# Output projection of an attention and S4D stack: float16 pairs with scales in place of split float32 pairs, and the normalised stream from ScalarE

## Chip, cores and metric

The kernel runs on one core of one Trainium2 chip. The metric is the device time of one execution in microseconds (us), the median over the runs shown. The profiler took one execution apart; times inside it count from the start of its span. Engines: PE is TensorE, PEld its weight loads, DVE is VectorE, ACT is ScalarE, POOL is GpSimd, SP is SyncE; SPq and POOLq are the queues from which SP and POOL issue transfers.

## What is computed

A stream x of 2048 rows by 640 columns goes through four layers, two of them attention (A) and two a state-space convolution (B), with the same weights each time:

```python
x = x + _A_ref(_layernorm(x), A_wqkv, A_wo)
x = x + _B_ref(_layernorm(x), B_log_A_real, B_A_imag, B_C_real, B_C_imag, B_log_dt, B_D_skip)
x = x + _A_ref(_layernorm(x), A_wqkv, A_wo)
x = x + _B_ref(_layernorm(x), ...)
```

A is attention with 32 heads of 20 columns: softmax of the scaled scores, times the values, and the result o, 2048 by 640, times the matrix wo, 640 by 640. That last product is the output projection, and it is what the change edits. B builds one filter of length 2048 for each of the 640 channels, convolves each channel with it by way of Fourier transforms, and adds the skip term.

## The kernel before

Rows of x are spread so that partition p holds rows 16p to 16p+15; a "row" s, 0 to 15, is one slice of 128 rows by 640 columns. A layer pair is attention (with the projection at its end), then the convolution, ssm; this happens twice, and the text calls them layer 1 and layer 2.

**Attention** runs blocks of four heads and 512 queries, 32 blocks a layer. Each block is 32 score tiles S of 128 by 1024 (scores, L769), one exp on ScalarE each into pt (L772), and the products of pt with the values into pa (values, L786), a pair of PSUM banks that exists once. At the end of a block VectorE copies pa to oc and adds the second bank (oc). The row sums then go through memory to be inverted and spread: POOL issues dn (four small stores from oc), dr (a load), VectorE inverts dr, POOL issues dn (a store) and db (four loads that spread it), VectorE multiplies oc by db, and POOL issues ot (four stores). Each of these steps has a due time in a planner's clock (the list later), and the wrapper Ordered (L74, the line that most VectorE, POOL and SP instructions carry) ties VectorE's instructions, and the transfers of POOL and SP, in the order in which they are recorded. POOL's arithmetic isn't tied: there a scheduler chooses the place.

**end_jobs** is called once a layer, when the side jobs of the attention are done. In layer 2 it checks the range of the weights wqkv by a maximum over all partitions (partition_all_reduce on POOL) and then calls **prefetch**, which loads wo into five tiles wot of 128 by 640 and splits each on POOL into two float32r halves: woh by a cast (L925), wol by a subtraction (L926). In layer 1 it loads x as well, in four transfers. POOL can hold the code of its arithmetic or that of the all-reduce; where it changes, the order of the instructions shows a row ISA with no operands.

**out_split** prepares one row of the attention's result: a load otl, a cast oh on ScalarE (L943), a subtraction ol on VectorE. **out_proj** takes the 16 rows in turn: for each half of 320 columns 15 matmuls into po (ol by woh, L1035; oh by woh and by wol, L1041), and VectorE adds po to x. Every two rows, and singly for the last two, ln_u makes the layer norm's output for the convolution: statistics on VectorE, u = (x - mean) * rs on VectorE, uh (float16) on ScalarE (L956), ul = u - uh on POOL (L957), for the last row on VectorE. The convolution's first matmuls (psx, L1100) read uh and ul. In layer 1 the transform of the filters, ktransform, is woven between the rows from row 2 on: it loads kl for 128 channels at a time, transposes and transforms (pkt, pkx, pkf), with copies out of PSUM on ScalarE and VectorE.

Line numbers are those of the profile.

## Time and profile before

| | before |
|---|---|
| median of 3 runs | 2904.78 us (2903.93 to 2905.59) |
| the profiled execution | 2906.51 us |
| its span | 2904.60 us |
| PE busy | 2581.2 us, 89% |
| ACT busy | 2360.6 us, 81% |
| DVE busy | 1497.7 us, 52% |
| POOL busy | 795.5 us, 27% |
| mean granted clock of TensorE | 0.98 |

The span is the time between the first and the last instruction on the core; 1.91 us of the execution lie outside it. A busy share is an average over the whole program, which has stages with different limits: in the attention loops ScalarE works without a pause, in the projections and the convolutions TensorE does. What a stage is worth is read from the stretch itself.

### The profile page before, as it was taken

The numbers are of one execution on the slowest core, as the hardware profiler recorded it, in microseconds if no ns is written. First come the engines' busy times: TensorE is split into PE (matmuls) and PEld (weight loads), VectorE is DVE, ScalarE is ACT, GpSimd is POOL, SyncE is SP. The second block draws the span as 40 slices with busy tenths as digits, with TensorE's granted clock in tenths as the row PEclk, the third lists the DMA queues.
The fourth block names the chain that finished last, engine by engine and source line by source line (L and its number), as shares of the span: only waits on it lengthen the run. The fifth ranks groups of instructions, "written<-read, shape, count | busy, mean of one in ns | idle before, by whom it ended". The sixth has DMA issues, their size and how long they took to land.

```text
span 2904.6 us, 127995 instructions
## 1 busy us (share of the span) xinstructions
PE 2581.2 (89%) x57088; PEld 1537.6 (53%) x57088; DVE 1497.7 (52%) x3333; ACT 2360.6 (81%) x2862; POOL 795.5 (27%) x1229
## 2 busy tenths in 40 slices
PE   7679898998999788789999898999999978878999
PEld 3235555554555444367788554544444433334988
DVE  8555667777775687146777633332222200001865
ACT  5878888998899788855565488999999989998364
POOL 1002223222222222330067012222222332222376
PEclk9889999999999999999999999999999999999999
DMA  5212222222111111335454212121211211112265
GB/s 165 105 55 58 62 59 60 62 53 68 52 55 42 51 41 50 131 119 185 190 188 140 67 35 64 55 65 40 61 46 44 66 28 39 31 43 61 86 204 162
DMA packets 174754, 231.45 MB, mean 80 GB/s; under 512 B 35952, under 2 KB 124336, under 8 KB 172400
## 3 DMA queue, kind: packets, MB, share of 16 engines
q1 hardware_dynamic: 139856, 180.84, 19.2%
q0 software_dynamic: 34336, 42.32, 5.8%
q8 instruction: 450, 7.37, 1.1%
q14 instruction: 112, 0.92, 0.1%
HBM read 150.94 MB, written 72.10 MB: 77 GB/s over the span
## 4 chain that ended last, share of the span: by engine, by line
ACT 26%; PE 18%; issue 6%; DMA 3%; DVE 2%; POOL 1%; SPq 0%; ACTq 0%; POOLq 0%; DVEq 0%
ACT pt L772 25%; PE psv L1135 2%; PE psy L1145 2%; PE po L1041 2%; PE psx L1123 2%; PE psx L1100 2%; PE pst L1110 1%; PE pkf L1015 1%; PE pkx L998 1%; PE pv L524 1%; PE po L1035 1%; PE pa L786 1%; PE pq L682 1%; DMA kl<-kd 1%; PE pkt L1007 1%
## 5 line engine op out<-in xcount | busy, mean ns | idle before, releaser
L772 ACT ACTIVATE pt<-S 128x1024 f32<-128x1024 f32 x2048 | 1932.4, 1040 | 168.2 <-PE S L769 155.1
L786 PE MATMUL pa<-pt,V 64*32 64x512 f32 x16384 | 1144.3, 597 | 17.3 <-DVE oc L74 9.3
L769 PE MATMUL S<-qop,kop 61*32 61x512 f16 x16384 | 921.8, 383 | 184.6 <-ACT pt L772 149.1
L769 PEld LDWEIGHTS <-kop 61*32 61x32 f16 x16384 | 393.8, 90 | 836.9 <-issue 742.5
L786 PEld LDWEIGHTS pa<-pt,V 64*32 64x32 f32 x16384 | 330.1, 107 | 93.7 <-issue 32.0
L74 POOL DMA_DIRECT2D dn<-oc x256 | 126.2, 499 | 446.2 <-DVE oc L74 352.4
L74 POOL DMA_DIRECT2D ot<-oc x256 | 129.2, 512 | 392.5 <-DVE oc L74 313.3
L74 DVE TENSOR_SCALAR qc<-m 128x512 f32<-128x512 f32 x64 | 44.2, 690 | 298.9 <-PE m L560 298.8
L322 PE MATMUL m<-kb,ka 64*32 64x64 f32 x10240 | 158.4, 222 | 44.6 <-issue 42.4
L322 PEld LDWEIGHTS m<-kb,ka 64*32 64x32 f32 x10240 | 150.8, 105 | 82.4 <-issue 65.3
L74 DVE COPY oc<-pa 128x512 f32<-128x512 f32 x64 | 44.2, 691 | 275.0 <-PE pa L786 275.0
L74 POOL DMA_DIRECT2D db<-dn x256 | 128.5, 508 | 133.7 <-DMA dn<-dr 126.0
L74 DVE TENSOR_TENSOR kb<-ktab 128x512 f32<-128x512 f32 x240 | 155.9, 684 | 16.4 <-PE m L322 16.4
L560 PE MATMUL m<-xh,wh 64*32 64x512 f16 x2560 | 148.8, 382 | 12.5 <-DVE qc L74 12.5
L560 PE MATMUL m<-xl,wh 64*32 64x512 f16 x2560 | 148.0, 381 | 0.0
L560 PE MATMUL m<-xh,wl 64*32 64x512 f16 x2560 | 147.0, 380 | 0.2 <-issue 0.2
L560 PEld LDWEIGHTS <-wh 64*32 64x32 f16 x5120 | 97.1, 94 | 79.0 <-issue 42.2
L1128 POOL TENSOR_TENSOR t<-t,kb 128x512 f32<-128x512 f32 x80 | 101.9, 1274 | 71.2 <-DVE t L74 70.3
L1112 ACT COPY xt<-pst 128x1024 f16<-128x1024 f16 x80 | 81.6, 1023 | 46.7 <-PE pst L1110 46.5
L74 DVE TENSOR_SCALAR dr<-dr 128x16 f32<-128x16 f32 x64 | 14.7, 229 | 188.5 <-DMA dr<-dn 188.4
L74 DVE TENSOR_TENSOR oc<-oc,db 128x512 f32<-128x512 f32 x64 | 44.1, 690 | 125.7 <-DMA db<-dn 124.2
L74 POOL DMA_DIRECT2D dn<-dr x64 | 35.6, 556 | 263.8 <-DVE dr L74 256.7
(222 smaller groups left out, 3877.3 us busy)
## 6 DMA issues: line engine op xcount, KB each, us to landing
ka<-kha SPq DMA_DIRECT2D x80, 256.0 KB
kb<-khb SPq DMA_DIRECT2D x80, 256.0 KB
db<-dn POOLq DMA_DIRECT2D x256, 64.0 KB, 2.6
qop<-qs SPq DMA_DIRECT2D x256, 40.0 KB
kop<-ks SPq DMA_DIRECT2D x128, 80.0 KB
ot<-oc POOLq DMA_DIRECT2D x256, 40.0 KB, 2.0
otl<-ot SPq DMA_DIRECT2D x32, 320.0 KB
kha<-kn SPq DMA_DIRECT2D x20, 512.0 KB
```

What stands on the lines that cost most here:

```text
L74: made = f(out, *a, **k)
L322: chain(te.matmul(ps[r][32 * j:32 * j + 32, c8, :], a[n // 2][rows, ch, :], b[n][rows, dd, :], start=(n == 0), stop=(n == 3), tile_positio ...
L560: chain(te.matmul(ps[r][32 * t:32 * t + 32, :], a_[rows, ct, 32 * t:32 * t + 32], m[rows, ct, sl], start=(k == 0), stop=(k == 14), tile_po ...
L769: chain(te.matmul(S[32 * t:32 * t + 32, 512 * r:512 * r + 512], kt_[rows, kc + 32 * t:kc + 32 * t + 32], qt[rows, :], start=True, stop=Tru ...
L772: se.activation(pt, S, AF.Exp, scale=SCALE)
L786: chain(te.matmul(pa[r][32 * j:32 * j + 32, :], V[rows, kt, VP * h:VP * h + 32], pts[j // 2][rows, 512 * (j % 2):512 * (j % 2) + 512], sta ...
L1041: te.matmul(pos[hf], oh[:, ct, :], m[:, ct, 320 * hf:320 * hf + 320], start=False, stop=(ct == NCT - 1 and m is wol))
L1100: te.matmul(ps[:, r, i, :], e1[:, e, s, r, :], m[:, s, bs], start=(n == 0), stop=(n == 2))
L1112: se.copy(xt, pt.rearrange("p k g c -> p k (g c)"))
L1123: te.matmul(px, f2[:, f, :], xt[:, k, :], start=(n == 0), stop=(n == 2))
L1128: ge.tensor_mul(t2, t2, kb)
L1135: te.matmul(pv[:, g].rearrange("p r i c -> p (r i c)"), t1[:, g * P:g * P + P], fa, start=True, stop=True)
```

## The change

wo is now split into float16 halves of 256 times wo (WS), and the rows of the attention into float16 halves of 16 times the row (OS): oh is an activation with a scale, ol one instruction that multiplies and subtracts. The sum into x multiplies po by 1 / (16 * 256) first. wot becomes one tile that lives as long as the projection; each of its five parts is scaled in place on POOL before the cast and the subtraction, and the splits are put on the list of due jobs (halves) behind the loads of x, all four of which are now on it as well. In layer 2 VectorE takes the maximum of each part of wot before it is scaled, and after the projection a second all-reduce checks the range (in_range, wom). ln_u makes u on ScalarE with a scale and a bias (nb).

```diff
 PB = 7
 AHEAD = ((0, 0.0), (108, 22.0), (364, 47.0), (490, 72.0), (740, 125.0))
 WS = 256.0
+OS = 16.0
 LG = 2
 BOUND = 30.0
 SCALE = DH ** -0.5
...
     hpi = cp.tile([P, 1], F32, name="hpi")
     ve.memset(hpi, math.pi / 2)
     flag = cp.tile([P, 2], F32, name="flag")
+    wom = cp.tile([P, NCT], F32, name="wom")
     warm = cp.tile([P, 1], F32, name="warm")
     ve.memset(flag, 0.0)
     with tc.tile_pool(name="op", bufs=1) as op:
...
         ve.tensor_scalar(t, t, -0.5, 1.5, ALU.mult, ALU.add)
         ve.tensor_mul(rs, rs, t)
         return rs
+
+    def in_range(wx, top):
+
+        ve.scalar_tensor_tensor(flag[:, 0:1], wx[:, 1:2], top, flag[:, 0:1], ALU.mult, ALU.max)
+        ve.reciprocal(wx[:, 0:1], wx[:, 1:2])
+        ve.tensor_scalar_mul(wx[:, 0:1], wx[:, 0:1], 2.0 ** -4)
+        ve.tensor_max(flag[:, 0:1], flag[:, 0:1], wx[:, 0:1])
 
     def exp_exact(pool, xx, n=D):
         k, r, q, z = (pool.tile([P, n], F32, name=f"ee_{t}{n}") for t in "krqz")
...
                 wx = sm.tile([P, 2], F32, name="wx")
                 ve.reduce_max(wx[:, 0:1], wm, axis=AX.X)
                 ge.partition_all_reduce(wx[:, 1:2], wx[:, 0:1], P, bass.bass_isa.ReduceOp.max)
-                ve.tensor_max(flag[:, 0:1], flag[:, 0:1], wx[:, 1:2])
-                ve.reciprocal(wx[:, 0:1], wx[:, 1:2])
-                ve.tensor_scalar_mul(wx[:, 0:1], wx[:, 0:1], 2.0 ** -4)
-                ve.tensor_max(flag[:, 0:1], flag[:, 0:1], wx[:, 0:1])
+                in_range(wx, 22.0)
             qc_.close()
             if not first_layer:
                 xpools.pop().__exit__(None, None, None)
             rest = []
-            made = prefetch(x, rest)
+            made = prefetch(x, rest, first_layer)
             later.extend((plan.pe + 8.0 + 3.0 * n, f) for n, f in enumerate(rest))
             later.sort(key=lambda e: e[0])
             return made
...
         c.close()
         return *tail[:-1], split, first
 
-    def prefetch(x, rest):
+    def prefetch(x, rest, first_layer):
 
         if x is None:
             xp = tc.tile_pool(name="xp", bufs=1, side="right")
...
                 rest.append(lambda i=i: sy.dma_start(x[:, i:i + 4, :], xv[:, i:i + 4, :]))
         c = ExitStack()
         w1 = c.enter_context(tc.tile_pool(name="wo1", bufs=1, side="right"))
-        woh = w1.tile([P, NCT, D], F32R, name="woh")
-        wol = w1.tile([P, NCT, D], F32R, name="wol")
-        with tc.tile_pool(name="wos", bufs=NCT, side="right") as ws:
-            for ct in range(NCT):
-                wt = ws.tile([P, D], F32, name="wot")
-                sy.dma_start(wt, wo[ct * P:ct * P + P, :])
-                ge.tensor_copy(woh[:, ct, :], wt)
-                ge.tensor_sub(wol[:, ct, :], wt, woh[:, ct, :])
-        if rest:
-            rest.pop(0)()
+        woh = w1.tile([P, NCT, D], F16, name="woh")
+        wol = w1.tile([P, NCT, D], F16, name="wol")
+        wt = w1.tile([P, NCT, D], F32, name="wot")
+        for ct in range(NCT):
+            sy.dma_start(wt[:, ct, :], wo[ct * P:ct * P + P, :])
+
+        def halves(ct):
+
+            if not first_layer:
+                ve.reduce_max(wom[:, ct:ct + 1], wt[:, ct, :], axis=AX.X, apply_absolute_value=True)
+            ge.tensor_scalar_mul(wt[:, ct, :], wt[:, ct, :], WS)
+            ge.tensor_copy(woh[:, ct, :], wt[:, ct, :])
+            ge.tensor_sub(wol[:, ct, :], wt[:, ct, :], woh[:, ct, :])
+        rest.extend(lambda ct=ct: halves(ct) for ct in range(NCT))
         return x, c, woh, wol, c.enter_context(tc.tile_pool(name="wo2", bufs=2, side="right"))
 
     def out_split(w2, n):
...
         o = []
 
         def split(s):
-            oh = w2.tile([P, NCT, P], F32R, name="oh")
-            ol = w2.tile([P, NCT, P], F32R, bufs=n, name="ol")
+            oh = w2.tile([P, NCT, P], F16, name="oh")
+            ol = w2.tile([P, NCT, P], F16, bufs=n, name="ol")
             cur = o.pop(0)
-            se.copy(oh, cur)
-            ve.tensor_sub(ol, cur, oh)
+            se.activation(oh, cur, AF.Copy, scale=OS)
+            ve.scalar_tensor_tensor(ol, cur, OS, oh, ALU.mult, ALU.subtract)
             if s + 1 < NI:
                 o.append(load(s + 1))
             return oh, ol
...
 
     def ln_u(x, i0, n, mvrs, uh, ul, pool):
         mv, rs = mvrs
+        nb = sm.tile([P, n], F32, tag="nb", name="nb")
+        ve.scalar_tensor_tensor(nb, mv[:, :, 0], -1.0, rs, ALU.mult, ALU.mult)
         for i in range(n):
             s = i0 + i
             u = pool.tile([P, D], F32, name="u")
-            ve.tensor_scalar(u, x[:, s, :], mv[:, i, 0:1], rs[:, i:i + 1], ALU.subtract, ALU.mult)
+            se.activation(u, x[:, s, :], AF.Identity, scale=rs[:, i:i + 1], bias=nb[:, i:i + 1])
             se.copy(uh[:, s, :], u)
             (ve if s == NI - 1 else ge).tensor_sub(ul[:, s, :], u, uh[:, s, :])
 
...
                         te.matmul(pos[hf], oh[:, ct, :], m[:, ct, 320 * hf:320 * hf + 320],
                                   start=False, stop=(ct == NCT - 1 and m is wol))
                 xs = x[:, s, 320 * hf:320 * hf + 320]
-                ve.tensor_add(xs, xs, pos[hf])
+                ve.scalar_tensor_tensor(xs, pos[hf], 1.0 / (OS * WS), xs, ALU.mult, ALU.add)
                 if s == 2:
                     weave(1000)
             if s >= NI - LG:
...
                         if n == 0:
                             filler[:] = ktransform(), 0.0, False
                         out_proj(x, *tail, ln)
+                        if n + 2 >= len(parts):
+                            wx = sm.tile([P, 2], F32, name="wx")
+                            ve.reduce_max(wx[:, 0:1], wom, axis=AX.X)
+                            ge.partition_all_reduce(wx[:, 1:2], wx[:, 0:1], P, bass.bass_isa.ReduceOp.max)
+                            in_range(wx, 1.0)
                 if not general:
                     wc.close()
                 c3.close()
```

The scheduler gives the recorded instructions their final order. Three places matter here.

POOL in layer 1, from the end of one block's stores (kd is a store of the filters) through the split; before:

```order
L74 DMA kd<-ko 128x8x64
L925 CAST woh<-wot 128x640
L74 DMA dn<-oc 16x1x32 x4
L926 ISA
L926 TENSOR_TENSOR wol<-wot,woh 128x640
L74 DMA dr<-dn 128x16
L925 CAST woh<-wot 128x640 x2
L926 TENSOR_TENSOR wol<-wot,woh 128x640 x2
L925 CAST woh<-wot 128x640
L74 DMA dn<-dr 128x16
```

The same place now:

```order
L75 DMA kd<-ko 128x8x64
L935 ISA
L935 TENSOR_SCALAR wot<-wot 128x640
L75 DMA dn<-oc 16x1x32 x4
L936 CAST woh<-wot 128x640
L935 TENSOR_SCALAR wot<-wot 128x640
L937 TENSOR_TENSOR wol<-wot,woh 128x640
L936 CAST woh<-wot 128x640
L75 DMA dr<-dn 128x16
L937 TENSOR_TENSOR wol<-wot,woh 128x640
L935 TENSOR_SCALAR wot<-wot 128x640 x2
L936 CAST woh<-wot 128x640 x2
```

The load of code has moved ahead of the first cast and of dn; two subtractions stand where three did before the store of the inverted sums (the second dn), and the scalings are new.

POOL in layer 2, from the all-reduce of the wqkv check; before:

```order
L74 ISA wx<-wx 128x1
L925 CAST woh<-wot 128x640
L926 ISA
L926 TENSOR_TENSOR wol<-wot,woh 128x640
L925 CAST woh<-wot 128x640 x2
L926 TENSOR_TENSOR wol<-wot,woh 128x640 x2
L925 CAST woh<-wot 128x640 x2
L926 TENSOR_TENSOR wol<-wot,woh 128x640 x2
L74 DMA dn<-oc 16x1x32 x4
L74 DMA dr<-dn 128x16
L74 DMA dn<-dr 128x16
L74 DMA db<-dn 32x512 x4
```

Now, from the same block's store of the inverted sums (ahead of it stand the all-reduce, dn, a load of code, dr and two of the five splits):

```order
L75 DMA dn<-dr 128x16
L935 TENSOR_SCALAR wot<-wot 128x640 x2
L936 CAST woh<-wot 128x640 x2
L937 TENSOR_TENSOR wol<-wot,woh 128x640 x2
L75 DMA db<-dn 32x512 x4
L935 TENSOR_SCALAR wot<-wot 128x640
L75 ISA
L75 ISA wx<-wx 128x1
L936 CAST woh<-wot 128x640
L75 DMA ot<-oc 20x512
L937 ISA
L937 TENSOR_TENSOR wol<-wot,woh 128x640
```

The second all-reduce, written after the projection, has moved into this block, between two loads of code.

VectorE in layer 2, the same block; before:

```order
L74 TENSOR_SCALAR fi<-flag 128x1
L74 COPY oc<-pa_49420 128x512
L74 TENSOR_TENSOR oc<-oc,pa_49421 128x512
L74 TENSOR_SCALAR dr<-dr 128x16
L74 RECIPROCAL dr<-dr 128x16
L74 TENSOR_TENSOR oc<-oc,db 128x512
L74 COPY oc<-pa_50130 128x512
```

Now, from the reciprocal of that block on:

```order
L75 RECIPROCAL dr<-dr 128x16
L75 TENSOR_REDUCE wom<-wot 128x1 x3
L75 TENSOR_REDUCE wx<-wom 128x1
L75 TENSOR_TENSOR oc<-oc,db 128x512
L75 SCALAR_TENSOR_TENSOR flag<-wx,flag 128x1
L75 RECIPROCAL wx<-wx 128x1
L75 TENSOR_SCALAR wx<-wx 128x1
L75 TENSOR_TENSOR flag<-flag,wx 128x1
L75 TENSOR_SCALAR fi<-flag 128x1
L75 COPY oc<-pa_50128 128x512
```

Between the multiply by db and the next block's copy of pa there are now five ops of one column; the first of them reads the result of the second all-reduce.

## Rows read from the trace of the kernel before

**Rows 1.** The page's chain that ended last, share of the span by engine.

```profile
ACT 26%; PE 18%; issue 6%; DMA 3%; DVE 2%; POOL 1%; SPq 0%; ACTq 0%; POOLq 0%; DVEq 0%
```

**Rows 2.** Timeline of ScalarE: start us, us, instruction [idle before <- what ended it].

```profile
1206.07 1.02 ACT L772 ACTIVATE pt<-S 128x1024 f32<-128x1024 f32 x1 [6.43 <-PE S L769]
...
2345.11 1.02 ACT L772 ACTIVATE pt<-S 128x1024 f32<-128x1024 f32 x1 [7.06 <-PE S L769]
```

**Rows 3.** Timeline of POOL in layer 1, the split of wo.

```profile
1166.80 0.96 POOL L74 DMA_DIRECT2D kd<-ko  x1 [1.94 <-DVE ko L74]
...
1173.80 1.97 POOL L74 DMA_DIRECT2D dn<-oc  x4
1184.23 1.55 POOL L926 TENSOR_TENSOR wol<-wot,woh 128x640 fp32r<-128x640 f32 x1 [8.46 <-issue]
...
1186.50 1.39 POOL L925 CAST woh<-wot 128x640 fp32r<-128x640 f32 x2
...
1196.59 2.02 POOL L74 DMA_DIRECT2D db<-dn  x4
```

**Rows 4.** Timeline of VectorE in layer 1, the same block and the next copy.

```profile
1187.75 3.86 DVE L74 TENSOR_SCALAR dr<-dr 128x16 f32<-128x16 f32 x1 [19.23 <-DMA dr<-dn]
...
1201.44 0.69 DVE L74 TENSOR_TENSOR oc<-oc,db 128x512 f32<-128x512 f32 x1 [9.55 <-DMA db<-dn]
...
1236.36 0.69 DVE L74 COPY oc<-pa 128x512 f32<-128x512 f32 x1 [10.10 <-PE pa L786]
```

**Rows 5.** Timeline of POOL in layer 2, the split of wo.

```profile
2301.73 0.32 POOL L74 PARTITION_ALL_REDUCE wx<-wx  x1
...
2314.08 1.54 POOL L926 TENSOR_TENSOR wol<-wot,woh 128x640 fp32r<-128x640 f32 x1 [9.84 <-issue]
...
2334.83 1.99 POOL L74 DMA_DIRECT2D db<-dn  x4 [1.65 <-DMA dn<-dr]
```

**Rows 6.** Timeline of VectorE in layer 2, the same block.

```profile
2302.09 0.16 DVE L74 TENSOR_TENSOR flag<-flag,wx 128x1 f32<-128x1 f32 x1 [2.62 <-POOL wx L74]
...
2305.41 0.69 DVE L74 COPY oc<-pa 128x512 f32<-128x512 f32 x1 [2.52 <-PE pa L786]
...
2340.74 0.69 DVE L74 COPY oc<-pa 128x512 f32<-128x512 f32 x1
```

**Rows 7.** Chain of waits in layer 2's projection: start us, us, what.

```profile
2696.18 2.68 DVE ol L74
...
2705.08 2.93 PE po L1041 x20
...
2709.48 2.93 PE po L1041 x20
```

**Rows 8.** Timeline of TensorE, values of layer 2 in float16.

```profile
1639.56 0.30 PE L524 MATMUL pv<-wv,xl 128*128 128x320 f16 x1
...
1641.60 0.30 PE L524 MATMUL pv<-wv,xl 128*128 128x320 f16 x1
```

**Rows 9.** Busy us (x instructions) in stretches, only what touches po.

```profile
1278.00:1308.00 30.00, 29.55 (x175) 28.46 (x175) 5.38 (x12) 0.89 0.51 171
1308.00:1452.00 144.00, 47.26 (x240) 36.05 (x240) 7.67 (x16) 1.00 0.49 187
...
2698.00:2748.00 50.00, 48.71 (x330) 48.41 (x330) 10.62 (x23) 1.00 0.20 60
```

**Rows 10.** Timelines of POOL and TensorE in layer 1's projection.

```profile
1287.66 3.66 POOL L957 TENSOR_TENSOR ul<-u,uh 128x640 f16<-128x640 f32 x2 [5.66 <-ACT uh L956]
...
1308.48 1.14 PE L990 MATMUL pkt<-ident,kl 128*128 128x128 f32 x8 [0.76 <-DVE kl L74]
```

**Rows 11.** Instructions by line and shape: busy us, mean ns of one.

```profile
L720 ACT ACTIVATE xn<-x,nb,rs 128x640 f32<-128x640 f32 x16 | 13.9, 915 | 0.8 <-DVE nb L74 0.8
```

**Rows 12.** DMA issues: count, KB each, median us from issue to landing.

```profile
dn<-oc POOLq DMA_DIRECT2D x256, 2.0 KB, 2.9
dr<-dn POOLq DMA_DIRECT2D x64, 8.0 KB, 2.0
```

## Prediction

> **What bounds the kernel now.** I read four views in this order. The page's chain of waits says which engine the end waits for: ScalarE leads, TensorE is second, and the waiting of the queues is small [rows 1]. ScalarE means the attention loop, where one exp instruction follows another; so whatever stops those exps lengthens the run one for one. The timeline of ScalarE shows two stops of 6.43 and 7.06 us, one in each attention [rows 2]. Both fall in the block after the weights of the output projection were split on POOL. That is the first surprise of this trace: the change edits exactly that split. TensorE is the second stretch: in the two output projections it runs almost without a gap, so there its pace counts.
>
> **What causes the two stops.** Each block of the attention ends with a chain through POOL's queue: dn (sums out), dr (sums in), reciprocal on VectorE, dn (back), db (spread), then VectorE multiplies oc by db. VectorE works in order, and behind that multiply stands the copy of the next block's pa. There is one pa in PSUM, so until that copy TensorE can't go on and ScalarE runs out of scores. In layer 1 POOL meets a load of code (the row ISA of the order) behind dn and idles 8.46 us before the first wol; four more wol and four casts stand before db, which starts at 1196.59 [rows 3]. VectorE's dr op took 3.86 us beside POOL's train of casts and subtractions, and the multiply came at 1201.44 [rows 4], the copy right behind it. In layer 2 the load was 9.84 us, db started at 2334.83 and the copy came at 2340.74 [rows 5, 6].
>
> **Part 1, the products of out_proj.** 480 matmuls a layer, 960 in all, count and columns unchanged; only their type changes. Before, 30 of them (one row of 16) take 4.40 us from one start to the next, 2705.08 to 2709.48, which is 146.7 ns each [rows 7]. A matmul of 320 float16 columns with 128 float16 weights stands in the trace already: 15 of them from 1639.56 to 1641.60, 136.0 ns each [rows 8]. So 10.7 ns each, 10.3 us at most. Not all of it stays, because two waits at the start of each projection hang on the last block's DMA chain. Layer 1: behind the wait for dr, 175 matmuls up to 1308 and 240 among the filter transform up to 1452 [rows 9]. The 175 give 1.9 us, and 0.76 us of waiting for kl goes too [rows 10]: that load waits for the ot stores, which stood behind two ul on POOL, 3.66 us from 1287.66 [rows 10]; the order now puts ot ahead of all ul, so kl can come about that much earlier. The 240 could give 2.6 us; part hides the kl loads of later units, and I take 1.6. Layer 2: 330 matmuls after the gate [rows 9], 3.5 us. One ol there took 2.68 us and held TensorE [rows 7]; what slowed it isn't visible, between 0 and 1.9 us go, and I take 0.8. Sum of part 1: 1.9 + 0.8 + 1.6 + 3.5 + 0.8 = 8.6 us.
>
> **Part 2, the normalised stream u on ScalarE.** 32 instructions leave VectorE. On ScalarE the same form costs 915 ns [rows 11], 29.3 us in all, under TensorE's 4.1 us a row: oh and uh, casts of the same 640 columns, are shorter, so the three stay below 2.8 us a row, and in layer 1 the copies of the filter transform come on top. I cost it at nothing there, with TensorE as cover. Without that cover, at the end of each projection, u lies on the path, and in layer 2 the last u now queues among casts of psx on ScalarE: 0.3 to 1 us, I take 0.8; in layer 1 it stands free, and I take 0.3 us gained since VectorE has less to do. Part 2 costs 0.5 us. oh with a scale, ol and the sum into x as one instruction keep their shape and I cost them at nothing.
>
> **Part 3, POOL's queue in layer 1.** The cast of before waits for wot, the load of code then follows dn. Now the load stands first and runs while wot comes. I take it at 9.15 us, the mean of 8.46 and 9.84. No scaling of this shape is in the trace; the nearest row is the cast, same shape, one input, 0.70 us (1.39 for two), and the upper end is the subtraction, 1.55 us [rows 3]. From the end of kd at 1167.76: load to 1176.9, scaling 1177.6, four dn to 1179.6, landing 2.9 us after the last was issued at 1179.1 [rows 12], 1182.0. POOL is meanwhile in cast, scaling, subtraction, cast until 1183.2; dr lands 2.0 us later [rows 12] but VectorE waits out the train (1.55 + 1.40 + 1.40 behind dr) as it did before, 1188.1; two small ops, 1188.6; dn back, about 2.1 us like dr, 1190.7; POOL's two subtractions, scaling, cast run to 1193.7, and db starts. The multiply follows 4.85 us after the start of db (1196.59 to 1201.44): 1198.6, so 2.8 us earlier. Between a scaling of 0.70 and of 1.55 us this ends at 2.8 us gained or 1.4 us lost.
>
> **Part 4, POOL's and VectorE's queues in layer 2.** dn now stands ahead of the load and the sums leave at 2307.2, right behind the copy at 2305.41 and its add; they left only behind all five splits before. Then load to 2318.3, scaling 2319.0, dr 2319.6, the train of 5.2 us to 2324.8, reciprocal 2325.3, dn 2325.9, a train of two scalings (each behind a maximum of wot on VectorE), two casts, two subtractions, some 6.2 us, to 2332.1: db starts 2.7 us earlier than before. But VectorE's queue has changed: between the multiply by db and the next copy of pa stand five one-column ops of 0.16 us [rows 6], the first of which waits for the second all-reduce, 0.32 us [rows 5], and that stands behind db (to 2334.1), the last scaling (2334.8) and another load of code. Behind the waiting VectorE stands the copy, and behind the copy TensorE and every exp. No row shows what a load for the all-reduce costs, since those of before fell into long idle times. Its bounds are 0 and 9.84 us; the nearest rows are the two loads for the subtraction, so 9.15 us: 2343.9, all-reduce 2344.3, five ops 2345.1, copy 2345.1. That is 4.4 us later than 2340.74. The third load, before the last wol, delays the next block's multiply to about 2373; in layer 1 the pa after the stopped block was full 34 us after the copy (1236.36 less 1202.1) [rows 4], so here near 2379, and that delay hides. TENSOR_LOAD fi on SP now waits to 2345 as well, with query loads behind it that are needed a block later: nothing.
>
> The row says 8.46 and 9.84 us for a load. The Trainium skill, "GPSIMD Engine Reference", section 2.1 on dispatch, gives about 6 us (5.95) for the first call into freshly loaded code; no row here agrees. By that figure layer 2 would gain about 2 us instead of losing 4.4, layer 1 some 5, and the sum would end near 2889.7, as an estimate.
>
> **The sum.** 8.6 - 0.5 + 2.8 - 4.4 = 6.5 us gained. The profiled execution took 2906.51 us (span 2904.60, 1.91 around it), so its like would take 2900.0; the median of the runs is 1.73 us below that execution, which gives **2898.3 us**.
>
> **Rivals.**
> *The all-reduce's code costs nothing to load* (the lower bound). Then VectorE waits for db alone: multiply at 2337.4, five ops, copy at 2339.0, 1.7 us earlier than before. 8.1 + 2.8 + 1.7 = 12.6 us: 2892.2. For it: nothing shows that load. Against: two loads out of two were long. Loads of about 6 us each, as "GPSIMD Engine Reference" of the Trainium skill has them, belong to this case and end a little below it.
> *Slower: POOL's train.* The ten added scalings cost what a two-input op does, 1.55 us, and loads 9.84. Layer 1 then loses 2.1 us (0.7 + 5 times 0.85 less 2.8), layer 2 loses 10.1 (4.4 + 1.4 + 4.3); against 8.1 that is 4.1 us lost: 2908.9. It decides from about 1.35 us a scaling, where all gain is gone. Against: a scaling reads one tensor, as the cast does.
> *ScalarE takes TensorE's gain.* A pair of u (1.83 us) and a pair of uh stand back to back before copies out of PSUM that the filter transform waits for. Five such places in layer 1, at about 1.1 us each past the slack, are 5.5 us: 2903.8. For it: the order does put them together; against: VectorE loses u at the same places, and ScalarE idles there now.
>
> **How the numbers follow.** The forecast 0.58, with 2894 to 2903 for itself (layer 2's loads each 0.7 us either way, the hidden 240 matmuls, the ol); cheap load 0.17; ScalarE 0.15; slower train 0.10. Some 0.2%, 5.8 us, is what a measurement can tell from no change; the forecast sits just past it, so a bit over half of its chance is faster, with the cheap load 0.49. Slower by more needs the train at its full price and some waiting besides: 0.06. The range reaches from below the cheap load to half way between the ScalarE case and the slow train.
>
> **What would show it.** Right: L1035 and L1041's successors start 136 ns apart; in layer 1 the multiply of the block after the split near 1198.6 and ScalarE's stop some 3 us shorter; in layer 2 POOL idle about 9 us before the all-reduce, VectorE's flag op waiting for it, and ScalarE's stop near 11 us; uh no later than before except in layer 2's last row. Wrong: a stop in layer 2 shorter than 7 us (cheap load), scalings over 1.3 us (slow train), or matmuls of out_proj that wait for VectorE or ScalarE more than now.

## Result and profile after

The changed kernel took 2918.34 us (median of 11 runs, 2909.94 to 2928.05) against 2904.78 us for the kernel before, beside it (11 runs, 2901.98 to 2911.30): a ratio of 1.0044, with a 95% interval of 1.0030 to 1.0058. So it is 12.8 us slower, where 6.5 us of gain were forecast; 2918.34 also lies above the forecast's range, whose upper end stands half way between the ScalarE case (2903.8) and the slow train (2908.9). Chips differ by a few microseconds, so what follows compares ratios to the kernel before on the same chip, and stretches inside a profile. A profile is one execution, so differences of one or two microseconds between two of them need a row that explains them. One of the 12 runs of experiment 6 took 3470.78 us at a mean granted clock of 0.71 and is left out of its ratio.

| from the profiled executions, us | before | after | forecast for the change |
|---|---|---|---|
| span | 2904.6 | 2916.3 | -6.5 |
| stop of ScalarE in layer 1 | 6.43 | 6.95 | -2.8 |
| po in layer 1, first wol product to last | 184.1 | 184.5 | -4.6 with its tail |
| stop of ScalarE in layer 2 | 7.06 | 11.15 | +4.4 |
| po in layer 2, first wol product to last | 70.2 | 75.6 | -3.5 with its tail |
| from there to the first pst | 10.7 | 12.5 | (in the line above) |

The profile page's chain of waits of the changed kernel hardly differs from [rows 1]; a loss of 0.4% doesn't show in such a view.

```profile
ACT 27%; PE 18%; issue 6%; DVE 2%; DMA 2%; POOL 1%; SPq 0%; ACTq 0%; DVEq 0%; POOLq 0%
```

ScalarE's timeline shows the two stops that answer to [rows 2]: the first did not shrink, the second grew by 4.1 us.

```profile
1208.42 1.02 ACT L781 ACTIVATE pt<-S 128x1024 f32<-128x1024 f32 x1 [6.95 <-PE S L778]
...
2349.81 1.02 ACT L781 ACTIVATE pt<-S 128x1024 f32<-128x1024 f32 x1 [11.15 <-PE S L778]
```

POOL's timeline in layer 2, to be laid beside [rows 5]: three loads of code (idle before the row), the middle one ahead of the second all-reduce.

```profile
2317.63 1.85 POOL L935 TENSOR_SCALAR wot<-wot 128x640 f32<-128x640 f32 x1 [7.88 <-PE S L778]
...
2344.16 0.38 POOL L75 PARTITION_ALL_REDUCE wx<-wx  x1 [5.77 <-issue]
...
2353.31 1.39 POOL L937 TENSOR_TENSOR wol<-wot,woh 128x640 f16<-128x640 f32 x1 [7.48 <-issue]
```

VectorE's timeline of the same block [rows 6] and, in its first row, the multiply of layer 1 [rows 4]: in layer 2 the multiply is done at 2339.3, and the copy of pa still stands until 2345.79, behind the flag op.

```profile
1203.80 0.69 DVE L75 TENSOR_TENSOR oc<-oc,db 128x512 f32<-128x512 f32 x1 [13.87 <-DMA db<-dn]
...
2338.62 0.69 DVE L75 TENSOR_TENSOR oc<-oc,db 128x512 f32<-128x512 f32 x1 [11.88 <-DMA db<-dn]
2344.57 0.65 DVE L75 SCALAR_TENSOR_TENSOR flag<-wx,flag 128x1 f32<-128x1 f32 x1 [5.26 <-POOL wx L75]
...
2345.79 0.69 DVE L75 COPY oc<-pa 128x512 f32<-128x512 f32 x1
```

What the split costs on POOL, by the view of the tile wot (shortest, median and longest in ns; first and last start): the added scaling is the dearest of the three.

```profile
L935 POOL TENSOR_SCALAR wot<-wot x10: 1811/1822/1850, 1177.2 to 2336.6; 128x640 f32<-128x640 f32 x10
L936 POOL CAST woh<-wot x10: 707/716/777, 1181.2 to 2344.4; 128x640 f16<-128x640 f32 x10
L937 POOL TENSOR_TENSOR wol<-wot,woh x10: 1393/1410/1421, 1183.7 to 2353.3; 128x640 f16<-128x640 f32 x10
```

The largest miss lies in the projection of layer 2. Of the kernel before, and then of the changed one, the view of the tile po gives first and last start of the wol products:

```profile
L1041 PE MATMUL po<-wol,oh x160: 308/309/310, 2677.1 to 2747.3; 128*128 128x320 f32 x160
```

```profile
L1053 PE MATMUL po<-wol,oh x160: 299/299/474, 2681.6 to 2757.2; 128*128 128x320 f16 x160
```

A row of 30 products now takes 4.08 us while nothing stops it, as forecast. But TensorE stops. Its timeline (only the longest stop, and one of three of that length, every second row):

```profile
2710.96 2.85 PE L1047 MATMUL po<-woh,ol 128*128 128x320 f16 x10 [4.36 <-DVE ol L75]
...
2731.24 1.53 PE L1047 MATMUL po<-woh,ol 128*128 128x320 f16 x10 [0.66 <-DVE ol L75]
```

The chain of waits tells the long one step by step (start, us, what):

```profile
2698.81 0.69 DVE oc L75
...
2702.29 1.29 DVE va L75
2704.04 0.89 DVE lt L75
...
2706.40 1.73 ACT u L967 x2
2708.65 0.72 ACT uh L968
2709.37 0.65 ACT oh L953
2710.04 0.87 DVE ol L75
2710.96 2.85 PE po L1047 x10
```

VectorE waits for the last block's db (until 2698.81); va and lt, ops of two columns, take 1.3 and 0.9 us; then u, u, uh, uh run on ScalarE, and the oh that TensorE needs stands behind them. After that stop the clock fell: the stretches of the po products (us, PE busy, DVE busy, granted clock, DMA share, GB/s) show 0.54 for the next 6 us, so mostly the lower of its two levels (1.2 and 2.4 GHz), with 25 products in 6.0 us of busy time where 275 took 37.8 behind it. At that pace (137 ns each) the 25 would take 3.4 us, so the clock cost 2.6 us.

```profile
2711.00:2717.00 6.00, 6.00 (x25) 0.96 (x2) 0.54 0.37 109
2717.00:2757.00 40.00, 37.77 (x275) 8.42 (x19) 1.00 0.17 51
```

In layer 1 the same op, va, takes 2.60 us while POOL subtracts two ul; the sum into x behind it is late, and TensorE waits for that. The timelines of VectorE, POOL and TensorE:

```profile
1291.04 2.60 DVE L75 TENSOR_SCALAR va<-mv 128x2 f32<-128x2 f32 x1
```

```profile
1290.84 2.77 POOL L969 TENSOR_TENSOR ul<-u,uh 128x640 f16<-128x640 f32 x2
```

```profile
1295.69 2.41 PE L1047 MATMUL po<-woh,ol 128*128 128x320 f16 x10 [1.85 <-DVE x L75]
```

Three questions followed. Is it u on ScalarE that costs the projection, by its order or by VectorE? Do the second all-reduce and POOL's arithmetic make the stops in the attention? And why do the runs of the changed kernel spread over 18 us?

### The profile page after: what moved, and what is told of

It reads as the page before. It is cut to its first block, busy times and chain, and to the rows that moved or that the text cites. A ratio compares the mean times of both kernels' runs of the same rounds, so it can differ in the third digit from the quotient of the medians.

```text
span 2916.3 us, 128040 instructions
## 1 busy us (share of the span) xinstructions
PE 2577.8 (88%) x57088; PEld 1491.3 (51%) x57088; DVE 1486.3 (51%) x3329; ACT 2385.2 (82%) x2894; POOL 814.7 (28%) x1240
## 3 DMA queue, kind: packets, MB, share of 16 engines
q8 instruction: 450, 7.37, 1.1%
## 4 chain that ended last, share of the span: by engine, by line
ACT 27%; PE 18%; issue 6%; DVE 2%; DMA 2%; POOL 1%; SPq 0%; ACTq 0%; DVEq 0%; POOLq 0%
ACT pt L781 26%; PE psv L1147 2%; PE psy L1157 2%; PE psx L1135 2%; PE psx L1112 2%; PE po L1053 1%; PE pkf L1027 1%; PE pv L533 1%; PE pst L1122 1%; PE pkx L1010 1%; PE pa L795 1%; PE pq L691 1%; PE po L1047 1%; PE pkt L1019 1%; DMA kop<-ks 1%
## 5 line engine op out<-in xcount | busy, mean ns | idle before, releaser
L778 PE MATMUL S<-qop,kop 61*32 61x512 f16 x16384 | 919.2, 383 | 184.1 <-ACT pt L781 147.9
L795 PEld LDWEIGHTS pa<-pt,V 64*32 64x32 f32 x16384 | 330.5, 107 | 99.0 <-issue 34.2
L75 DVE TENSOR_SCALAR dr<-dr 128x16 f32<-128x16 f32 x64 | 14.0, 219 | 184.1 <-DMA dr<-dn 184.1
```

What stands on the lines that cost most here:

```text
L75: made = f(out, *a, **k)
L778: chain(te.matmul(S[32 * t:32 * t + 32, 512 * r:512 * r + 512], kt_[rows, kc + 32 * t:kc + 32 * t + 32], qt[rows, :], start=True, stop=Tru ...
L795: chain(te.matmul(pa[r][32 * j:32 * j + 32, :], V[rows, kt, VP * h:VP * h + 32], pts[j // 2][rows, 512 * (j % 2):512 * (j % 2) + 512], sta ...
```

## Experiments

In the table po is layer 2, first product (ol by woh) to last; each comes from the view of the tile po of its profile. The ratios of most rows overlap, so the theories are judged by the stretches more than by the totals.

| kernel | ratio to before (95%) | po, layer 2 | stops of ScalarE, layers 1 and 2 |
|---|---|---|---|
| before | 1 | 71.9 | 6.43, 7.06 |
| the change | 1.0044 (1.0030 to 1.0058) | 77.1 | 6.95, 11.15 |
| before, u on ScalarE | 1.0025 (1.0014 to 1.0035) | 77.5 | 6.02, 3.90 |
| change, u on VectorE | 1.0031 (1.0014 to 1.0047) | 69.8 | 7.37, 11.28 |
| change, oh first | 1.0039 (1.0026 to 1.0052) | 73.1 | 6.92, 11.34 |
| change, ul of 4 rows on VectorE | one run only | 73.2 | 12.98, 11.20 |
| change, one all-reduce | 1.0028 (1.0014 to 1.0042) | 76.6 | 13.31, 6.04 |
| change, split on VectorE | 0.9994 (0.9983 to 1.0006) | 76.9 | 7.27, none |

**1. Only u moves.** The kernel before with ln_u of the change:

```diff
-            ve.tensor_scalar(u, x[:, s, :], mv[:, i, 0:1], rs[:, i:i + 1], ALU.subtract, ALU.mult)
+            se.activation(u, x[:, s, :], AF.Identity, scale=rs[:, i:i + 1], bias=nb[:, i:i + 1])
```

> The kernel before with one thing of the change: u on ScalarE with a scale and a bias; wo and o stay float32 pairs. Theory A (u on ScalarE costs the projection by itself): the order u, u, uh, uh, oh stops TensorE at any pace; po of layer 2 grows from 71.9 to 77 us or more, the tail behind it from 7.0 to about 9 us, and the time is 2911 to 2916 us. Theory C (at the old pace of 4.40 us a row the loop through ScalarE still fits, only the faster float16 rows wait for it): po of layer 2 stays at 72 to 74 us, only the tail grows, and the time is 2904 to 2908 us.

po took 77.5 us, so theory A holds and C falls: even at the old pace the move costs 5.6 us there, and the ratio is 1.0025. ScalarE's timeline shows the order, and TensorE's the stop that it ends in:

```profile
2702.69 1.73 ACT L957 ACTIVATE u<-x,nb,rs 128x640 f32<-128x640 f32 x2 [2.60 <-DVE nb L74]
2704.33 1.34 ACT L958 CAST uh<-u 128x640 f16<-128x640 f32 x2
2705.57 1.35 ACT L943 CAST oh<-otl 128x640 fp32r<-128x640 f32 x2
```

```profile
2707.24 3.03 PE L1037 MATMUL po<-woh,ol 128*128 128x320 f32 x10 [3.96 <-DVE ol L74]
```

The whole lost 7.3 us by the ratio, within theory A's range. In the profiled execution po gives 5.6 and the tail 1.0 of it (11.7 us to the first pst); ScalarE's stop in layer 2 was 3.90 us instead of 7.06, but the first po product of layer 1 began 2.9 us later than before with no edited instruction ahead of it. Neither was followed up. The chain to the long stop also holds a va of 1.38 and an lt of 0.90 us, as in the change, so order alone is not shown to cost the whole 5.6 us; experiments 3 and 4 part the two.

**2. The other way round: the change with u on VectorE** (the two lines of experiment 1 swapped, nb gone).

> The change with u = (x - mean) * rs made on VectorE again, as before; all else of the change stays. Theory A (the order on ScalarE): in the projections oh, which TensorE needs next, stands behind u, u, uh, uh on ScalarE, in layer 2 for 4.66 us once and 0.96 us every second row. Then the po matmuls of layer 2, 77.1 us from the first start to the last in the change, take 67 to 69 us here, the half-clock stretch inside them goes, the tail behind them is some 2 us shorter, and the whole is 9 to 13 us shorter than the change: 2904 to 2909 us. Theory B (VectorE is what is late there, with its sums, subtractions and statistics; ScalarE only passes the delay on): VectorE has more to do now, so the stop stays or grows, po takes 76 us or more, and the time is 2916 us or more.

In layer 2 theory A holds: po took 69.8 us, 0.8 above its bounds, the tail (to the first pst) 11.4 us, 1.1 less, and the stops every second row are gone. The time did not follow, 1.0031 instead of a ratio near 1.001. In the profiled execution layer 1 gave it back: po there ran from 1262.6 to 1453.6, 191.0 us where the change has 186.0. POOL's timeline has two ul ahead of the ot stores, as in the kernel before [rows 10], and kl comes late, which TensorE's row shows (the change has no wait for kl there):

```profile
1283.80 3.63 POOL L967 TENSOR_TENSOR ul<-u,uh 128x640 f16<-128x640 f32 x2 [4.42 <-ACT uh L966]
1287.38 2.01 POOL L75 DMA_DIRECT2D ot<-oc  x4
```

```profile
1306.33 2.99 PE L1000 MATMUL pkt<-ident,kl 128*128 128x128 f32 x12 [3.40 <-DVE kl L75]
```

That explains 3.4 of the 5 us; TensorE's waits for kx within the filter transform grew too, from 2.9 to 4.8 us. One long stop of 2.90 us also stayed in layer 2, so order is not its only cause: the ol ahead of it took 2.66 us, with one of POOL's subtractions (1.41 us) beside it.

**3. The change with oh ahead of u**, by recording each layer norm one row later:

```diff
+            while late:
+                ln(*late.pop())
...
-                ln(s + 1 - LG, LG)
+                late.append((s + 1 - LG, LG))
```

> The change with the layer norm of two rows recorded one row later, behind the split of the next row, so that on ScalarE an oh stands ahead of the u of its pair; u stays on ScalarE and no instruction is added. Theory A (the order on ScalarE): the 4.66 us stop and the 0.96 us every second row go, po of layer 2 takes 67 to 70 us instead of 77.1, and the whole is 6 to 10 us shorter than the change: 2907 to 2912 us. Theory B (VectorE is late): nothing changes, po 76 us or more and 2915 us or more. A third one, that ScalarE has too much work whatever its order, gives the same as B for po but with ScalarE busy without a pause there.

Half of theory A stands: the stops every second row went (rows of 4.08 us), but one long stop stayed, and po took 73.1 us. The timelines of VectorE, POOL and TensorE show what it waits for:

```profile
2692.11 2.98 DVE L75 TENSOR_SCALAR va<-mv 128x2 f32<-128x2 f32 x1
2695.01 0.81 DVE L75 SCALAR_TENSOR_TENSOR ol<-otl,oh 128x640 f16<-128x640 f32 x1
```

```profile
2692.31 2.75 POOL L969 TENSOR_TENSOR ul<-u,uh 128x640 f16<-128x640 f32 x2
```

```profile
2695.88 2.85 PE L1048 MATMUL po<-woh,ol 128*128 128x320 f16 x10 [4.88 <-DVE ol L75]
```

An op of two columns that takes 0.17 us elsewhere lasted until both of POOL's subtractions were done, at 2695.06, and the ol behind it was late. So theory B has a part too, and the next kernel tests it.

**4. The change with ul of four rows on VectorE**, so that POOL does no arithmetic there:

```diff
-            (ve if s == NI - 1 else ge).tensor_sub(ul[:, s, :], u, uh[:, s, :])
+            (ve if s == NI - 1 or s < 4 else ge).tensor_sub(ul[:, s, :], u, uh[:, s, :])
```

> The change with ul of the first four rows subtracted on VectorE instead of POOL. Theory L (a small VectorE op with both its tensors in SBUF stands still while POOL's subtraction runs): the op va of rows 2 and 3 in layer 2, 1.37 us in the change (2.98 in the run with oh first) takes about 0.17, the next lt 0.16 instead of 0.88, and TensorE's stop of 4.66 us shrinks by about 2 us less what the extra subtractions cost. Against it: a VectorE op of 1.3 us or more stays there with no POOL arithmetic beside it.

Theory L holds. VectorE's row of that va, and the stop of TensorE that was 4.36 us:

```profile
2711.94 0.15 DVE L75 TENSOR_SCALAR va<-mv 128x2 f32<-128x2 f32 x1
```

```profile
2710.23 1.53 PE L1047 MATMUL po<-woh,ol 128*128 128x320 f16 x10 [1.79 <-DVE ol L75]
```

No row of this stretch shows the lower clock, and po took 73.2 us although u, u, uh, uh still stand ahead of oh. In layer 1 va took 0.16 instead of 2.60 us, TensorE's wait of 1.85 us behind it became 0.46, and po took 180.7 us, where two executions of the change took 186.0 and 183.8 (experiment 7): part of the missing gain there was the same hold. The total of this single run is not read, since its stop in layer 1 was a long one, 12.98 us (experiment 7).

**5. The change with one all-reduce:** the block `wx = ...; in_range(wx, 1.0)` after the projection is left out.

> The change without the second all-reduce and the four range ops behind it (the range check of wo is left out). Theory A (the load of the all-reduce's code, then VectorE's wait for it): the copy of pa in layer 2 stands behind the multiply by db alone, near 2339.3 instead of 2345.8; ScalarE's stop of 11.15 us falls to about 4.5, and the time by 6 to 7 us: 2910 to 2912 us. Theory B (POOL's train of scalings is what holds the block): the stop falls by under 1 us and the time is 2916 us or more.

ScalarE's stop in layer 2 fell by 5.1 us to 6.04, 1.5 above the expectation; 0.8 of that is the multiply itself, which took 1.48 us instead of 0.69, again beside a subtraction of POOL.

```profile
2344.78 1.02 ACT L781 ACTIVATE pt<-S 128x1024 f32<-128x1024 f32 x1 [6.04 <-PE S L778]
```

```profile
2339.37 1.48 DVE L75 TENSOR_TENSOR oc<-oc,db 128x512 f32<-128x512 f32 x1 [13.15 <-DMA db<-dn]
```

The time fell less, to 1.0028, and its stop in layer 1, where nothing was edited, was 13.31 us. Experiment 7 takes that up.

**6. The change with the split on VectorE:**

```diff
-            ge.tensor_scalar_mul(wt[:, ct, :], wt[:, ct, :], WS)
-            ge.tensor_copy(woh[:, ct, :], wt[:, ct, :])
-            ge.tensor_sub(wol[:, ct, :], wt[:, ct, :], woh[:, ct, :])
+            ve.tensor_scalar_mul(woh[:, ct, :], wt[:, ct, :], WS)
+            ve.scalar_tensor_tensor(wol[:, ct, :], wt[:, ct, :], WS, woh[:, ct, :], ALU.mult, ALU.subtract)
```

> The change with the split of wo on VectorE: one scaling cast and one multiply-and-subtract for each of the five parts, none on POOL. Theory A (POOL's loads of code and its train hold dn, dr and db): both loads in the attention go, ScalarE's stops of 6.95 and 11.15 us fall to under 2 us each, and the time falls by 13 to 18 us: 2899 to 2904 us. Theory B (any engine that does the split holds the copy of pa, since VectorE works in order and has ten or fifteen more ops of 0.6 to 0.8 us): stops of 4 us or more stay, and the time is 2908 us or more.

Theory A holds for the two stops: the loads and the train were what made them. In layer 2 there is none, 147 exps in one piece, and the ratio is 0.9994, 12 to 15 us below the two measurements of the change.

```profile
2284.50 135.96 ACT L781 ACTIVATE pt<-S 128x1024 f32<-128x1024 f32 x147
...
1217.04 1.36 ACT L952 ACTIVATE oh<-otl 128x640 f16<-128x640 f32 x2 [7.27 <-DMA dn<-dr]
```

The second row is a new stop in layer 1, which theory A did not expect: the first oh stand ahead of exps on ScalarE and wait for otl, which SP issued at 1201.90 behind the 5.2 MB of x (1198.83). The row names a dn as what came last, but oh reads otl alone, so that it is otl is inferred here; experiments 8, 9 and 11 name it. The oh had stood behind the stop before.

**7. The change once more.**

> The change itself once more, on the chip of the two runs beside it. Theory D (in layer 1 the loads of x, 5.2 MB that SP issues within 2 us of POOL's db, sometimes get ahead of it): ScalarE's stop in layer 1 is either about 7 us (db issued 2 us before the first x) or about 13 us (issued at the same time), and the runs spread over more than 10 us. If the spread has another source, the stop is 7 us in whatever run.

The ratio was 1.0035 (1.0023 to 1.0047), 2915.33 to 2927.42 us over 12 runs. In the change, and in the kernels above that keep its split and its loads of x, POOL's db and SP's loads of x meet in layer 1; the timelines give (the second column is POOL's idle time ahead of the first scaling, for the load of code and for wot):

| kernel | idle before the scaling | db issued | first x issued | later by | db issue to multiply | stop |
|---|---|---|---|---|---|---|
| u on VectorE | 7.59 | 1194.06 | 1196.39 | 2.33 | 5.83 | 7.37 |
| oh first | 7.70 | 1186.69 | 1188.90 | 2.21 | 5.26 | 6.92 |
| the change | 7.66 | 1198.58 | 1200.72 | 2.14 | 5.22 | 6.95 |
| the change again | 8.46 | 1202.57 | 1203.91 | 1.34 | 8.49 | 11.02 |
| one all-reduce | 9.35 | 1194.90 | 1195.39 | 0.49 | 9.92 | 13.31 |
| ul of 4 rows on VectorE | 9.38 | 1206.03 | 1206.44 | 0.41 | 9.54 | 12.98 |

Theory D fits: in six executions in which the same lines issue the two, the stop follows how far db is ahead of x. The second column says what moves. Counted from the end of kd, x is issued 31.1 to 31.2 us later in all six, and db 28.9 to 30.7 us later, by as much as POOL idles longer. So 1.7 us more of that idle time go with a stop some 6 us longer: 1.7 us come directly, and over 4 us because db then meets x. Why the idle time varies is open. It fits the spread, but other sources take part: the profiled run of the change is a mild case, and at 2918.05 us it still lies at the median of its runs.

**8. The change with x loaded later,** behind the first otl:

```diff
+            loads, rest = (rest[:-NCT], rest[-NCT:])
             later.extend((plan.pe + 8.0 + 3.0 * n, f) for n, f in enumerate(rest))
+            later.extend((plan.pe + 45.0 + 3.0 * n, f) for n, f in enumerate(loads))
```

> The change with the four loads of x recorded 37 us later, behind the first load of otl. Theory D: db in layer 1 lands within 5 us of its issue, the stop there is 4 to 7 us in every run, and the median is 2 to 7 us below that of the change on the same chip, with a narrower spread. Without a collision to avoid: the same time within 2 us, or longer, since otl and x now load later in the last block.

This was a miss: 1.0059 (1.0044 to 1.0075), slower than the kernel before and no faster than the change. With x out of the way the multiply did come 5.52 us after the issue of db, as theory D has it, but the stop moved to the first oh on ScalarE, which now waits for an otl that SP issued only at 1213.03:

```profile
1216.46 0.74 ACT L955 ACTIVATE oh<-otl 128x640 f16<-128x640 f32 x1 [11.43 <-DMA otl<-ot]
```

**9. A version that keeps the float16 pairs.** It has u and the split on VectorE and the later x (the diffs of experiments 2, 6 and 8). Besides, a one-column subtraction on POOL, behind the ot stores of one block of each layer, loads the code of the arithmetic in idle time, and the first two ul are tied behind ot:

```diff
+                    if blk == (26 if first_layer else 29):
+                        ge.last = tie(ge.engine.tensor_sub(gw[:, 0:1], gw[:, 1:2], gw[:, 1:2]), ge.last)
...
-            (ve if s == NI - 1 else ge).tensor_sub(ul[:, s, :], u, uh[:, s, :])
+            made = (ve if s == NI - 1 else ge).tensor_sub(ul[:, s, :], u, uh[:, s, :])
+            if s < 2 and ge.last is not None:
+                tie(made, ge.last)
```

> Float16 pairs as in the change; u on VectorE; the split of wo on VectorE; the loads of x recorded 37 us later, behind the first loads of otl; one small POOL subtraction behind an earlier store in each layer, so that the code of the arithmetic is loaded while POOL is idle; ul of rows 0 and 1 tied behind the last ot. If all three places are what costs (ScalarE's order in the projection, POOL's loads and train in the attention, otl behind the x loads): ScalarE's stops under 2 us in both layers, po of layer 2 67 to 70 us, and the time 2883 to 2891 us. If the split on VectorE only moves the stop (as the 8.6 us that stayed in layer 1 with the split on VectorE may say): a stop of 5 us or more in layer 1 and 2894 us or more.

It took 0.9961 (0.9946 to 0.9976), which would be 2893.5 us beside the 2904.78 of the kernel before, 2.5 us above the expectation: po 69.1 us, no stop in layer 2, but 4.47 us in layer 1 where the load of code (9.73 us) held dn, and 3.32 and 1.66 us for otl.

**10. The same with u on ScalarE behind oh** (the later layer norm of experiment 3).

> As the run before it, but u stays on ScalarE, and the layer norm of two rows is recorded one row later, so that oh stands first. VectorE has less to do and TensorE's tail is longer: po of layer 2 68 to 73 us, the tail 9 us, and 2886 to 2894 us. If ScalarE's work in the projection is no cost once its order is right, this is within 3 us of the run with u on VectorE.

It took 0.9981 (0.9969 to 0.9993). The two intervals overlap, but on the same chip the medians are 2906.81 and 2899.77 us, and the stretches agree: po 71.9 us, 2.8 more than with u on VectorE, and 13.3 us from there to the first pst, 2.0 more. So in the two orders tried u on ScalarE is a cost.

**11. Experiment 9 with the load of code in layer 1 one step later,** behind the db of block 27, and the first split 8 us later in the plan:

```diff
+                    if blk == 27 and first_layer:
+                        ge.last = tie(ge.engine.tensor_sub(gw[:, 0:1], gw[:, 1:2], gw[:, 1:2]), ge.last)
...
-                    if blk == (26 if first_layer else 29):
+                    if blk == 29 and not first_layer:
...
-                    later.extend(((plan.pe + 7.0, fetch), (plan.pe + 20.0, lambda: first.append(split(0)))))
+                    later.extend(((plan.pe + 7.0, fetch), (plan.pe + 28.0, lambda: first.append(split(0)))))
```

> The kernel with float16 pairs, u on VectorE, the split on VectorE and the later loads of x, with two stops mended that it still had in layer 1: the small POOL subtraction stands behind an earlier db (12 to 15 us of idle POOL follow there) instead of behind ot, where the load of code held dn and cost ScalarE 4.47 us, and the first oh is recorded 8 us later, where it cost 3.32 and 1.66 us of waiting for otl. Both gone: 6 to 9 us less than that kernel, 16 to 20 us below the kernel before. If the stops only move on to the next engine: 3 us or less gained on it.

It took 0.9946 (0.9931 to 0.9961), about 16 us below the kernel before, the lowest ratio of the study, with po 68.7 us. The stop at the load of code is gone; 3.17 and 2.70 us of waiting for otl stayed, so of the 6 to 9 us hoped for about 4 came, and these 4 lie within the two intervals, which touch.

## Why the prediction was wrong

**Part 1, products.** The pace was right: 4.08 us a row, 10.6 us in all at most. "Layer 2: 330 matmuls after the gate, 3.5 us" failed, since TensorE was no longer the cover: it stopped 4.36 us once, 0.66 us on each of three rows and 0.25 on one, and its clock cost another 2.6 us. In layer 1 "1.9 + 0.8 + 1.6" came out as -0.4, and as 1.8 in the second execution of the change (182.3 us). kl did come earlier (no wait for it is left), but TensorE's waits for x grew from 2.8 to 5.5 us, 1.85 of them behind the held va (0.46 without POOL's subtractions, experiment 4); the rest is not accounted for. What the prediction could not see, why an ol took 2.68 us [rows 7], the trace of the kernel before shows on POOL: a subtraction lies inside it, and the ol ends 0.7 us behind it.

```profile
2696.74 1.41 POOL L957 TENSOR_TENSOR ul<-u,uh 128x640 f16<-128x640 f32 x1
```

**Part 2, u on ScalarE.** This is the step that failed most: "I cost it at nothing there, with TensorE as cover", from a sum of busy times of 2.8 us in a row of 4.1. Busy time was not the question. oh stands behind u in ScalarE's order, u waits for VectorE's statistics, and two rows of u and uh come at once; experiment 1 prices it at 5.6 us in layer 2 with no float16 at all. In the change that order and POOL's hold on VectorE have about equal shares: po falls from 77.1 by 4.0 us with oh first, by 3.9 with POOL's subtractions moved, and by 8.0 in experiment 9. The tail cost 1.8 us where 0.8 was taken. The rival "ScalarE takes TensorE's gain" came nearest, but had u and uh hold up copies of the filter transform, in layer 1 alone and for 5.5 us.

**Part 3, POOL in layer 1.** The load of code did move ahead of dn, but a scaling took 1.82 us, not 0.70, above even the upper bound of 1.55. Five of them ahead of db are 5.6 us more than forecast; the load (at most 7.66 us, forecast 9.15) and the dr op (done 3.9 us after the issue of dr, forecast 4.9) gave back 2.5. The multiply came at 1203.80, not at 1198.6. Of these 5.2 us 1.8 are not the split's: kd ended at 1169.58, where the kernel before has 1167.76, with no edited instruction ahead of it. From there the multiply took 34.2 us, forecast 30.8, before 33.7. The rival "slower: POOL's train" named this, with layer 1 losing 2.1 us; 0.5 were lost.

**Part 4, POOL and VectorE in layer 2.** The path was right: VectorE's flag op waited for the second all-reduce behind another load, and the copy stood behind it. The copy at 2345.79 (forecast 2345.1) and ScalarE's stop of 11.15 us (near 11) came so near by luck, since two errors cancelled: db went out at 2334.46 instead of 2332.1 and the scaling behind it took 1.83 us, and the load for the all-reduce took 5.77 us where 9.15 was taken. The sentence on the Trainium skill ("GPSIMD Engine Reference", section 2.1, about 6 us) fits this load, but not the two for the arithmetic in the same stretch, 7.88 and 7.48 us.

By parts the forecast missed by 10.7 us in layer 2's projection with its tail, 4.7 in layer 1's po (its tail, 14.6 and then 14.2 us, came as forecast) and 3.3 in layer 1's stop, less 0.4 elsewhere: 18.3 in all. The two spans miss it by 18.2, and the ratio by 19.3. Single executions do not warrant such agreement: the 1.8 us of part 3 were down to 0.6 at layer 2's block, and a second execution of the change has 2.2 us less in layer 1's po and 4.1 us more in its stop. Layer 2's po repeats, 75.6 and 75.7 us.

## What to carry to other kernels

Before an operation is moved to an engine with idle time, look at what stands behind it in that engine's order and when its input comes: pairs of 0.9 us activations ahead of a 0.7 us cast that TensorE waits for cost 5.6 us here, on an engine that was busy for 22 of 72 us before. Look also at when a transfer that gates the bottleneck is issued against bulk loads from another queue: here 2.1 us ahead of 5.2 MB was enough, and 1.3 us was not. And where a rare instruction makes POOL load code, put that load where POOL idles long enough for it: a one-column subtraction did that in experiment 11.

## What the runs showed of the hardware

- A VectorE op with its operands in SBUF can be held until POOL's arithmetic beside it ends, however small it is: two columns took 2.98 us beside two ul of 2.75 us, and 0.15 without them. The Trainium skill, "SBUF — State Buffer", section "SBUF: two separate sides", says that GpSimd shares a port pair with those VectorE ops that run in a 2-port mode or read two SBUF tensors, that whichever starts first holds it for a whole instruction, and that the other waits. These rows agree that one waits; no view names the mode of an op, and which came first they do not settle, as the row of that va opens 0.20 us ahead of POOL's. [rows 4] had it already, in the dr op of 3.86 us. Not every op is held: beside the two ul of 2720.11 in the change, the statistics of 320 columns took their usual 0.48 us and ol 0.86 us, and POOL was the later one (3.34 us for the pair instead of 2.75).
- On POOL a scaling of 128x640 float32 in place took 1.82 us, more than a subtraction of two such tiles into float16 (1.41 us) and two and a half times a cast (0.72 us). The cause was not looked for.
- POOL idled 5.8 to 6.1 us for the load of code before the all-reduce of the split's block, in six executions, and 7.1 to 10.3 us before arithmetic; in layer 1 the latter can hold some waiting for wot.
- 5.2 MB issued 0.4 to 1.3 us behind a 256 KB transfer went with 8.5 to 9.9 us from its issue to the multiply that reads it, and issued 2.1 to 2.3 us behind with 5.2 to 5.8 us.
